# The last batch's PSUM banks, its maxima and the buffers around it laid out anew in an attention plus soft-MoE kernel

## The chip, the cores and the metric

The kernel runs on one NeuronCore of a Trainium2 chip. The engines that matter are PE (TensorE, with its weight loads shown apart as PEld), DVE (VectorE), ACT (ScalarE), POOL (GpSimd) and SP (SyncE, which here only issues DMAs). PE writes only to PSUM, which has eight banks of 512 float32 values on each of 128 partitions; DVE and ACT read PSUM and write SBUF; DMA moves data between HBM and SBUF.

The metric is the device time of one execution in microseconds. The time before is the median of three runs. Separately one execution was profiled; its span runs from its first to its last instruction.

## The reference

Twelve heads of causal attention over 8 batches of 448 tokens, followed by a soft mixture of 8 experts with 4 slots each. `x` is the attention output with all heads of a token side by side, 3584 tokens by 768.

```python
scores = np.where(mask, -1e9, q @ k.T / sqrt(64))
attn = np.exp(scores - scores.max(-1)); attn /= attn.sum(-1) + 1e-09
x = (attn @ v)                       # 8 x 448 tokens, 12 heads x 64 = 768 columns
logits = x @ phi                     # 3584 x 32 slots
d = np.exp(logits - logits.max(0)); d /= d.sum(0) + 1e-09      # over the tokens
slot_input = d.T @ x                 # 32 x 768, 4 slots for each of 8 experts
slot_out[e] = np.maximum(slot_input[e] @ w1[e], 0) @ w2[e]     # 768 -> 1024 -> 768
c = np.exp(logits - logits.max(1)); c /= c.sum(1) + 1e-09      # over the slots
out = c @ slot_out
```

The softmax `d` runs over all tokens, so no expert can start before the last batch's logits are known.

## The kernel before

**Attention.** The 96 heads (`NHD`) are worked off in one loop, `i` from 0 to 96, with an order written out by hand in `ORDER`; what is issued keeps program order on each engine (`_InOrder`). In step `i` PE makes the scores of head `i + 2` and `attv(i - 1)`, twenty products of the exponentials `pt_[(i-1) % 2]` with the values `va_`, into the PSUM tile `po0`; `norm` divides and stores into `x`. Pairs of heads `p = i // 2` share a column block of 128; six pairs make a batch. Three buffers `x_` hold three pairs each in turn, so the last batch lies in `x_[2]` (pairs 42 to 44) and `x_[0]` (pairs 45 to 47), and `x_[1]` holds the second half of the batch before. `plan` hangs the mixture's work on steps of the loop: `xtrans(p)` transposes a pair's `x` into an `xt` tile (PE, then an ACT copy), `logits_a` multiplies it with `phi`, `logits_b` takes the negated maximum of a batch and the running one, `logits_d` the exponentials, `dispatch` adds `d.T @ x` to the slot inputs `si`.

**The last batch.** Step 95 runs `attv(94)`, the plan's `xtrans(46)` and opens three score tiles as `ps`; step 96 runs `attv(95)` into `ps[0]`, of which lines 540 to 542 first clear a part, because the last chunk of tokens writes 65 rows. Lines 543 to 602 then finish batch 7 outside the loop:

- `lp` (in `ps[1]`) gets the partial logits `lt` by a product with the identity, pair 46's by `logits_a`, and pair 47's behind four transposes into `xp` (in `ps[2]`), which ACT copies out in one half (`xa`) and DVE in the other (`mx_`, the attention's buffer for maxima);
- `logits_b` and `logits_d` run on `lp`; `tm` takes the transposed running maximum, DVE reduces it over four groups of tokens into `nm` and copies it three times in one instruction; one product spreads it over the partitions, and `wc`, `rz`, `sidw` rescale the groups;
- `dispatch_a` multiplies into `sps` (right parts of `ps[2]` and `ps[0]`), `dispatch_b` adds into `si`, `tps` gathers the slot inputs into `slt`, and `zr` the denominators;
- the logits are copied to `lt`, transposed and copied to `lg[:, 7]`, which only the combine stage reads.

`warm(n, w)` issues `n` products whose result nobody reads, 512 columns wide, between these steps.

**Experts and output.** `expert_in(e)` is 24 x 4 products of `slt` with the first weights, `expert_out(e, hf)` 8 of the hidden values with the second; `combine` makes the output tiles in two halves of columns, and SP stores them.

**The weight stream.** `order` lists 64 weight loads, all issued by SP in program order, each into one tile of 1536 columns. Loads 0 to 21 go to `wres` during the attention. Loads 22 to 33 (line 678) go to the pool `wt1`, which takes the SBUF that `early.close()` frees: each load waits for the last use of whatever its 6144 bytes per partition lay on. Loads 34 to 63 reuse tiles 0 to 29 and wait for the expert products that read them. The pools on the right side lie one behind the other, later ones at lower addresses, tiles in the order of their declaration. Worked out from the declared sizes, the loads lie on these tiles before:

| load | lies on |
|---|---|
| 27 | `r2` of even pairs, `k2` of odd pairs |
| 28 | `k2`, `r2` of odd pairs, `mx` |
| 29 | `mx`, `mt`, `va0`, `pt0` |
| 30 | `pt0`, `va1`, `pt1` |
| 31 | `pt1`, small tiles, both `xt` |
| 32 | `xt`, `x1` |
| 33 | `x1`, `lt`, `x0` |
| 34 to 37 | weight tiles 0 to 3, read by `expert_in(0)` |

```python
    x_[1] = moe.tile([P, NCH, 3 * P], F32, name="x1")
    lt = moe.tile([P, P], F32, name="lt")
    x_[0] = moe.tile([P, NCH, 3 * P], F32, name="x0")
    x_[2] = moe.tile([P, NCH, 3 * P], F32, name="x2")
```

Of the kernel before, what the change touches and what calls it, by code (L numbers as in the profile page):

```python
# [9 lines left out]
F32 = mybir.dt.float32  # L10
# [24 lines left out]
WARM = (1, 2, 3, 1)  # L35
# [44 lines left out]
def attention_soft_moe(ctx: ExitStack, tc: tile.TileContext, qk, va, phi, w1, w2, out):  # L80
# [10 lines left out]
    ps_s = att.enter_context(tc.tile_pool(name="ps_s", bufs=3, space=PSUM))  # L91
    ps_1 = att.enter_context(tc.tile_pool(name="ps_1", bufs=1, space=PSUM))

# [8 lines left out]
    x_[1] = moe.tile([P, NCH, 3 * P], F32, name="x1")  # L102
# [75 lines left out]
    def warm(n, w=None):  # L178

        w = misc("warm") if w is None else w  # L180
        for _ in range(n):
            nc.tensor.matmul(w, identb, tri.unsqueeze(1).to_broadcast([P, 4, P]),
                             start=True, stop=True)
# [115 lines left out]
    def attv(i, qcs, first):  # L299
        if not 0 <= i < NHD:  # L300
            return
        p, h = divmod(i, 2)
        pt, v, po = pt_[i % 2], va_[p % 2], st.get(("po", i), po0)
        for qc in qcs:
            for c in range(qc + 1):
                col = SCOL[c] + P * (qc - c)


                m = P if qc < 3 else 65
                nc.tensor.matmul(po[0:m, qc], pt[:, col:col + m], v[:, c, h],  # L310
                                 start=c == 0 and qc in first, stop=c == qc, skip_group_check=True)
# [101 lines left out]
    for b in range(NB):  # L413
        o, last = 12 * b, b == NB - 1
        for j, r in enumerate((3, 5, 8, 9, 11, 13)):
            if not last or j < PPB - 1:
                plan[o + r] = lambda p=b * PPB + j: xtrans(p)
        plan[o + 10] = lambda b=b: next_logits(b, 2, misc(f"g{b}_2"))
        if not last:
            plan[o + 14] = lambda b=b: (next_logits(b, 4, misc(f"g{b}_4")), logits_b(b, lt))  # L420
            plan[o + 16] = lambda b=b: logits_e(b)
            plan[o + 18] = lambda b=b: dispatch(b, 0)
            plan[o + 19] = lambda b=b: dispatch(b, 1)
# [45 lines left out]

    def sid_part(g):  # L470
        nc.gpsimd.affine_select(out=sid, in_=sid, compare_op=ALU.not_equal, fill=1.0,
                                base=-32 * g, pattern=[[-1, NSLOT]], channel_multiplier=1)
# [4 lines left out]
    later += [lambda g=g: sid_part(g) for g in range(4)]  # L477

# [3 lines left out]
    for i in range(NHD + 1):  # L482
# [55 lines left out]
        if i == NHD - 1:  # L538

            ps = [ps_s.tile([P, 1024], F32, tag="s", name=f"e{k}") for k in range(3)]  # L540
            po = st["po", i] = ps[0][:, 0:NCH * VC].rearrange("p (c n) -> p c n", n=VC)
            nc.vector.memset(po[64:P, 3], 0.0)
    b = NB - 1
    lp, xp, tm, wm = ps[1][:, 0:P], ps[2][:, 0:512], misc("tm"), ps[1][:, 512:1024]

    nc.tensor.matmul(lp, ident, lt, start=True, stop=False, skip_group_check=True)
    logits_a(b, (4,), lp, first=False, last=False)
    warm(WARM[0], wm)
    x = st.pop(("x", NPAIR - 1))
    for c in range(NCH):  # L550
        nc.tensor.transpose(out=xp[:, P * c:P * c + P], in_=x[:, c], identity=ident)
    xa = xtp.tile([P, 512], F32, tag="xt", name="xta", bufs=2)
    nc.scalar.activation(out=xa[:, 0:256], in_=xp[:, 0:256], func=AF.Copy)
    nc.vector.tensor_copy(out=mx_[:, 0:256], in_=xp[:, 256:512])
    warm(WARM[1], wm)
    for c in range(NCH):
        nc.tensor.matmul(lp[32 * c:32 * c + 32], phis[1][:, 2], (xa if c < 2 else mx_)[:, P * (c % 2):P * (c % 2) + P],
                         start=False, stop=True, skip_group_check=True)
# [5 lines left out]
    nm = const.tile([1, 4, NSLOT], F32, name="nm")  # L564
    nc.vector.tensor_reduce(out=nm[:, 0], in_=tm[0:1, 0:P].rearrange("p (c s) -> p s c", s=NSLOT),
                            axis=AX.X, op=ALU.min)
    nc.vector.tensor_copy(out=nm[:, 1:4], in_=nm[:, 0:1].to_broadcast([1, 3, NSLOT]))
    nc.tensor.transpose(out=xp[:, 0:P], in_=gs, identity=ident)
    dn = st["dn", b] = gs.rearrange("p (c s) -> p c s", s=NSLOT)
    nc.scalar.activation(out=gs, in_=xp[:, 0:P], func=AF.Copy)  # L570
    nc.tensor.matmul(tm[:, P:P + 1], nm.rearrange("p c s -> p (c s)"), ident[0:1, 0:1], start=True, stop=True)
# [5 lines left out]
    sps = ps[2][:, 512:896], ps[0][:, 512:896]  # L577
# [7 lines left out]
    for hf in range(2):  # L585
        tps = (po0 if hf == 0 else po).rearrange("p a b->p (a b)")[:, 0:3 * NSLOT]
        for c in range(3):
            o = 384 * hf + P * c
            nc.tensor.matmul(tps[:, NSLOT * c:NSLOT * c + NSLOT], si[:, o:o + P], sidw,
                             start=True, stop=True)  # L590
        if hf == 0:
            nc.scalar.activation(out=slt[0], in_=tps, func=AF.Copy)
            zr = misc("zr")[:, 0:1]
            nc.tensor.matmul(zr, srep.rearrange("p a b->p (a b)"), rz, start=True, stop=True)
        else:
            nc.vector.tensor_copy(out=slt[1], in_=tps)

    nc.vector.tensor_scalar(out=rz, in0=zr, scalar1=EPS, scalar2=None, op0=ALU.add)
    nc.vector.reciprocal(out=rz, in_=rz)
    nc.scalar.activation(out=lt, in_=lp, func=AF.Copy)  # L600
    nc.tensor.transpose(out=xp[:, P:2 * P], in_=lt, identity=ident)
    nc.scalar.activation(out=lg[:, b], in_=xp[:, P:2 * P], func=AF.Copy)
# [126 lines left out]
    for e in range(NEXP):  # L729
        expert_in(e)  # L730
        loads(4)
# [66 lines left out]
```

## Time and profile before

| what | value |
|---|---|
| time, median of 3 runs | 467.52 us (466.68 to 469.02) |
| the profiled execution's own time | 468.74 us |
| its span | 467.0 us |
| PE, PEld busy | 428.3 us (92%), 363.3 us (78%) |
| DVE, ACT, POOL busy | 354.5, 329.8, 266.0 us |
| granted PE clock, mean | 0.983 |
| HBM read, written | 107.25 MB, 11.01 MB |

How to read it: busy shares are means over two stages. Up to about 360 us the attention keeps PE busy; behind it the weights and the output go through the DMA queue. The parts of the profile that carry the argument are quoted where it uses them. A row of the chain or the timeline gives the start in us, the duration in us, the engine and what is written from what; "x8" counts merged instructions, and the bracket behind gives the idle time before and what ended it. A row of a windows view gives the stretch, its length, then for PE, PEld, DVE, ACT and POOL the busy time with the number of instructions, the granted PE clock, the DMA share and GB/s.

### The profile page before, as it was taken

Reading aid. Unit: us, or ns where it says so; the run is one execution under the profiler, and the core shown is the slowest. Engines: PE = TensorE matmul, PEld = TensorE weight load, DVE = VectorE, ACT = ScalarE, POOL = GpSimd, SP = SyncE. Lnnn points to the kernel's source line nnn. Section 1 sums busy time; section 2 is a strip of 40 time slices with the busy share of each in tenths; the row PEclk is TensorE's granted clock in tenths of the full one; section 3 lists DMA queues with packets and bytes.
Section 4 is the critical chain, followed back from the end, with each engine's and each line's share of the span. In section 5 each row is a group of like instructions: output and inputs, shape, how many; then the busy total and the mean of one; then the engine's idle time right before and its main releaser. Section 6 shows DMA issues by size and latency. Waiting matters only on the chain.

```text
span 467.0 us, 11997 instructions
## 1 busy us (share of the span) xinstructions
PE 428.3 (92%) x4567; PEld 363.3 (78%) x4567; DVE 354.5 (76%) x1053; ACT 329.8 (71%) x489; POOL 266.0 (57%) x214
## 2 busy tenths in 40 slices
PE   6999999999999999999999999999999898976640
PEld 3699999999899989998999999899988454622220
DVE  5898899888988988898899888988985466322350
ACT  5798888889889979897888889789965111422240
POOL 4789778677777777876777777777771000000000
PEclk9999999999999999999999999999999999999985
DMA  7477766777667765767766677666748699999997
GB/s 240 130 253 233 231 193 222 230 232 218 198 207 233 236 225 171 242 217 232 215 216 201 225 234 232 204 197 223 247 149 314 239 413 413 416 414 413 403 394 287
DMA packets 38200, 119.03 MB, mean 255 GB/s; under 512 B 4096, under 2 KB 11776, under 8 KB 38144
## 3 DMA queue, kind: packets, MB, share of 16 engines
q1 hardware_dynamic: 38000, 118.01, 73.5%
q8 instruction: 36, 0.59, 0.5%
q10 hardware_dynamic: 144, 0.27, 0.1%
q14 instruction: 20, 0.16, 0.1%
HBM read 107.25 MB, written 11.01 MB: 253 GB/s over the span
## 4 chain that ended last, share of the span: by engine, by line
PE 68%; DMA 15%; ACT 5%; DVE 4%; issue 2%; POOL 1%; SPq 0%; ACTq 0%; POOLq 0%
PE po L64 29%; PE s L64 23%; DMA w<-in_w_dram 13%; PE xt L64 5%; PE sp L64 3%; PE g L64 2%; PE rt L64 2%; ACT pt L64 2%; DMA out_dram<-ot 2%; PE e L64 2%; ACT ks L64 2%; DMA qk<-in_qk_dram 1%; DVE mx L64 1%; PE pp L64 1%; ACT ot L64 1%
## 5 line engine op out<-in xcount | busy, mean ns | idle before, releaser
L64 PE MATMUL po<-va,pt 128*128 128x65 f32 x1900 | 193.6, 250 | 0.0
L64 PEld LDWEIGHTS po<-va,pt 128*128 128x128 f32 x1900 | 190.6, 171 | 0.3 <-DVE x L64 0.2
L64 DVE TENSOR_TENSOR mx<-s,mx 128x320 f32<-128x320 f32 (+2 forms) x288 | 100.8, 350 | 28.8 <-ACT mx L64 25.2
L64 POOL TENSOR_TENSOR r<-qk,qd 64x896 fp32r<-64x896 f32 (+1 forms) x50 | 101.4, 2029 | 7.6 <-ACT qd L64 3.8
L64 POOL TENSOR_SCALAR_AFFINE_SELECT r<-mr 14x448 fp32r<-14x448 f32 x96 | 61.4, 640 | 76.3 <-DVE mr L64 68.5
L64 ACT ACTIVATE pt<-s 128x1024 f32<-128x1024 f32 x96 | 98.0, 1021 | 7.4 <-PE s L64 3.8
L64 POOL TENSOR_TENSOR ks<-qk,ks 64x896 fp32r<-64x896 f32 (+1 forms) x47 | 98.0, 2084 | 5.0 <-ACT ks L64 1.4
L64 PE MATMUL s<-r,k 128*128 128x320 f32 (+3 forms) x384 | 83.2, 299 | 1.1 <-POOL r L64 1.1
L64 PE MATMUL s<-qd,ks 128*128 128x448 f32 (+3 forms) x384 | 78.0, 314 | 2.0 <-ACT qd L64 1.9
L64 ACT ACTIVATE mx<-s 128x448 f32<-128x448 f32 x96 | 52.4, 546 | 34.5 <-PE s L64 16.9
L64 DVE STREAM_TRANSPOSE mt<-mx 128x448 f32<-128x448 f32 x96 | 61.9, 645 | 3.3
L64 PEld LDWEIGHTS s<-r,k 128*128 128x128 f32 (+1 forms) x384 | 60.1, 176 | 5.2 <-issue 1.6
L64 PEld LDWEIGHTS s<-qd,ks 128*128 128x128 f32 (+1 forms) x384 | 56.3, 184 | 3.6 <-ACT qd L64 2.8
L64 DVE TENSOR_REDUCE r<-mt 128x14 f32<-128x448 f32 x96 | 58.4, 608 | 0.1
L64 ACT ACTIVATE ks<-qk 128x896 fp32r<-128x896 f32 (+1 forms) x50 | 45.6, 914 | 3.3 <-DMA qk<-in_qk_dram 3.3
L64 ACT ACTIVATE qd<-qk 128x896 fp32r<-128x896 f32 (+1 forms) x50 | 46.1, 923 | 0.9 <-DMA qk<-in_qk_dram 0.8
L64 ACT ACTIVATE k<-ks 64x896 fp32r<-64x896 f32 (+1 forms) x49 | 45.8, 934 | 1.1
L64 PEld LDWEIGHTS <-identb 128*128 128x128 bf16 x312 | 29.0, 103 | 19.1 <-issue 15.4
L64 DVE TENSOR_TENSOR x<-po,sm 128x256 f32<-128x256 f32 x95 | 40.3, 424 | 3.3
L64 PE MATMUL s<-tri,identb 128*128 128x64 bf16 (+2 forms) x288 | 40.3, 237 | 0.9
L64 PE MATMUL so<-w,ht 128*32 128x384 f32 x256 | 25.3, 493 | 9.4 <-DMA w<-in_w_dram 7.3
L64 ACT ACTIVATE xts<-xt 128x512 f32<-128x512 f32 x47 | 28.1, 598 | 7.2 <-PE xt L64 4.2
(129 smaller groups left out, 399.0 us busy)
## 6 DMA issues: line engine op xcount, KB each, us to landing
w<-in_w_dram SPq DMA_DIRECT2D x64, 768.0 KB, 9.0
qk<-in_qk_dram SPq DMA_DIRECT2D x94, 448.0 KB, 3.4
va<-in_va_dram SPq DMA_DIRECT2D x47, 260.0 KB, 3.5
out_dram<-ot SPq DMA_DIRECT2D x28, 384.0 KB, 6.6
qk<-in_qk_dram SPq DMA_DIRECT2D x4, 224.0 KB, 3.7
va<-in_va_dram ACTq DMA_DIRECT2D x1, 260.0 KB, 5.2
phi<-in_phi_dram SPq DMA_DIRECT2D x2, 48.0 KB, 3.7
```

The costliest lines, as they stand in the source:

```text
L64: return self._tc.keep_in_program_order(op(*args, **kwargs))
```

## The change

Everything lies in and around the last batch.

- **Banks.** The pool of the single PSUM tiles (`ps_1`) is declared ahead of the score tiles. After step 95 the score pool is closed and six single banks `e0` to `e5` are opened in its place: `xp` becomes two banks, `po`, `lp` and the two `sps` one each. `warm` writes into `po0`, 256 columns wide; `WARM` goes from 7 products in all to 15.
- **No memset.** In the last head the weights of the last chunk are 128 columns wide instead of 65, so that all rows are written, and the clearing goes.
- **Order.** `xtrans(46)` moves out of the plan of step 95 to behind `attv(95)`, and its `logits_a` behind the copies of pair 47.
- **Transposes in one buffer.** Both halves of pair 47's transposes go to `xa`; `mx_` isn't used there.
- **Maxima.** `nm` is 128 x 128, cleared once by POOL in a step of the loop; DVE writes its first row, and four products of 32 columns spread it in place of a copy and one product.
- **Late steps.** The last logits are copied to `nm` instead of `lt`; their transposition and the copy to `lg` move behind `expert_in(0)`, into a tile of the output pool; `zr` moves behind the slot inputs.
- **Layout.** `x1` moves from `moe` to the front of `xtp`. By the same arithmetic as above loads 28 to 30 lie where they lay; load 31 lies on `pt1`, small tiles and `x1`; load 32 on `x1` and both `xt`; load 33 on an `xt`, `lt` and `x0`.

```diff
-WARM = (1, 2, 3, 1)
+WARM = (3, 3, 6, 3)
...
-    ps_s = att.enter_context(tc.tile_pool(name="ps_s", bufs=3, space=PSUM))
     ps_1 = att.enter_context(tc.tile_pool(name="ps_1", bufs=1, space=PSUM))
+    scs = ExitStack()
+    ps_s = scs.enter_context(tc.tile_pool(name="ps_s", bufs=3, space=PSUM))
...
-    x_[1] = moe.tile([P, NCH, 3 * P], F32, name="x1")
+    x_[1] = xtp.tile([P, NCH, 3 * P], F32, name="x1")
...
-            nc.tensor.matmul(w, identb, tri.unsqueeze(1).to_broadcast([P, 4, P]),
+            nc.tensor.matmul(w, identb, tri.unsqueeze(1).to_broadcast([P, w.shape[1] // P, P]),
...
-                m = P if qc < 3 else 65
+                m = P if qc < 3 or i == NHD - 1 and c < 3 else 65
...
-            if not last or j < PPB - 1:
+            if not last or j < PPB - 2:
                 plan[o + r] = lambda p=b * PPB + j: xtrans(p)
...
+    nm = const.tile([P, P], F32, name="nm")
...
+    later += [lambda: nc.gpsimd.memset(nm[:, 0:NSLOT], 0.0)]
...
-            ps = [ps_s.tile([P, 1024], F32, tag="s", name=f"e{k}") for k in range(3)]
-            po = st["po", i] = ps[0][:, 0:NCH * VC].rearrange("p (c n) -> p c n", n=VC)
-            nc.vector.memset(po[64:P, 3], 0.0)
+            scs.close()
+            pe = att.enter_context(tc.tile_pool(name="pe", bufs=1, space=PSUM, reuse_waits="tile"))
+            ps = [pe.tile([P, 512], F32, name=f"e{k}") for k in range(6)]
+            po = st["po", i] = ps[2][:, 0:NCH * VC].rearrange("p (c n) -> p c n", n=VC)
     b = NB - 1
-    lp, xp, tm, wm = ps[1][:, 0:P], ps[2][:, 0:512], misc("tm"), ps[1][:, 512:1024]
+    xtrans(NPAIR - 2)
+    xp, lp, sps = ps[0:2], ps[3][:, 0:P], [ps[k][:, 0:384] for k in (4, 5)]
+    tm, wm = misc("tm"), po0.rearrange("p a b->p (a b)")[:, 0:2 * P]
 
     nc.tensor.matmul(lp, ident, lt, start=True, stop=False, skip_group_check=True)
-    logits_a(b, (4,), lp, first=False, last=False)
     warm(WARM[0], wm)
     x = st.pop(("x", NPAIR - 1))
     for c in range(NCH):
-        nc.tensor.transpose(out=xp[:, P * c:P * c + P], in_=x[:, c], identity=ident)
+        nc.tensor.transpose(out=xp[c // 2][:, P * (c % 2):P * (c % 2) + P], in_=x[:, c], identity=ident)
...
-    nc.scalar.activation(out=xa[:, 0:256], in_=xp[:, 0:256], func=AF.Copy)
-    nc.vector.tensor_copy(out=mx_[:, 0:256], in_=xp[:, 256:512])
+    nc.scalar.activation(out=xa[:, 0:256], in_=xp[0][:, 0:256], func=AF.Copy)
+    nc.vector.tensor_copy(out=xa[:, 256:512], in_=xp[1][:, 0:256])
+    logits_a(b, (4,), lp, first=False, last=False)
     warm(WARM[1], wm)
     for c in range(NCH):
-        nc.tensor.matmul(lp[32 * c:32 * c + 32], phis[1][:, 2], (xa if c < 2 else mx_)[:, P * (c % 2):P * (c % 2) + P],
+        nc.tensor.matmul(lp[32 * c:32 * c + 32], phis[1][:, 2], xa[:, P * c:P * c + P],
                          start=False, stop=True, skip_group_check=True)
...
-    nm = const.tile([1, 4, NSLOT], F32, name="nm")
-    nc.vector.tensor_reduce(out=nm[:, 0], in_=tm[0:1, 0:P].rearrange("p (c s) -> p s c", s=NSLOT),
+    nc.vector.tensor_reduce(out=nm[0:1, 0:NSLOT], in_=tm[0:1, 0:P].rearrange("p (c s) -> p s c", s=NSLOT),
                             axis=AX.X, op=ALU.min)
-    nc.vector.tensor_copy(out=nm[:, 1:4], in_=nm[:, 0:1].to_broadcast([1, 3, NSLOT]))
...
-    nc.tensor.matmul(tm[:, P:P + 1], nm.rearrange("p c s -> p (c s)"), ident[0:1, 0:1], start=True, stop=True)
+    for c in range(NCH):
+        nc.tensor.matmul(tm[32 * c:32 * c + 32, P:P + 1], nm[:, 0:NSLOT], ident[:, 0:1],
+                         start=True, stop=True, skip_group_check=True)
...
-    sps = ps[2][:, 512:896], ps[0][:, 512:896]
...
-            zr = misc("zr")[:, 0:1]
-            nc.tensor.matmul(zr, srep.rearrange("p a b->p (a b)"), rz, start=True, stop=True)
         else:
             nc.vector.tensor_copy(out=slt[1], in_=tps)
+    nc.scalar.activation(out=nm, in_=lp, func=AF.Copy)
+    zr = misc("zr")[:, 0:1]
+    nc.tensor.matmul(zr, srep.rearrange("p a b->p (a b)"), rz, start=True, stop=True)
...
-    nc.scalar.activation(out=lt, in_=lp, func=AF.Copy)
-    nc.tensor.transpose(out=xp[:, P:2 * P], in_=lt, identity=ident)
-    nc.scalar.activation(out=lg[:, b], in_=xp[:, P:2 * P], func=AF.Copy)
...
         expert_in(e)
+        if e == 0:
+            lgp = pso.tile([P, 512], F32, tag="o", name="lgp")
+            nc.tensor.transpose(out=lgp[:, 0:P], in_=nm, identity=ident)
+            nc.scalar.activation(out=lg[:, NB - 1], in_=lgp[:, 0:P], func=AF.Copy)
```

More of the change, by code (lines that the diff above doesn't have):

```diff
@@ L563, in attention_soft_moe @@
     logits_d(b, lp)
-    nm = const.tile([1, 4, NSLOT], F32, name="nm")
-    nc.vector.tensor_reduce(out=nm[:, 0], in_=tm[0:1, 0:P].rearrange("p (c s) -> p s c", s=NSLOT),
+    nc.vector.tensor_reduce(out=nm[0:1, 0:NSLOT], in_=tm[0:1, 0:P].rearrange("p (c s) -> p s c", s=NSLOT),
                             axis=AX.X, op=ALU.min)
-    nc.vector.tensor_copy(out=nm[:, 1:4], in_=nm[:, 0:1].to_broadcast([1, 3, NSLOT]))
-    nc.tensor.transpose(out=xp[:, 0:P], in_=gs, identity=ident)
+    nc.tensor.transpose(out=xp[0][:, 0:P], in_=gs, identity=ident)
     dn = st["dn", b] = gs.rearrange("p (c s) -> p c s", s=NSLOT)
-    nc.scalar.activation(out=gs, in_=xp[:, 0:P], func=AF.Copy)
-    nc.tensor.matmul(tm[:, P:P + 1], nm.rearrange("p c s -> p (c s)"), ident[0:1, 0:1], start=True, stop=True)
+    nc.scalar.activation(out=gs, in_=xp[0][:, 0:P], func=AF.Copy)
+    for c in range(NCH):
+        nc.tensor.matmul(tm[32 * c:32 * c + 32, P:P + 1], nm[:, 0:NSLOT], ident[:, 0:1],
+                         start=True, stop=True, skip_group_check=True)
     warm(WARM[3], wm)
```

## The prediction

> **What bounds the kernel now.** I read the page's slices first, for the rows that leave the attention's pattern.
>
> ```profile
> DMA  7477766777667765767766677666748699999997
> GB/s 240 130 253 233 231 193 222 230 232 218 198 207 233 236 225 171 242 217 232 215 216 201 225 234 232 204 197 223 247 149 314 239 413 413 416 414 413 403 394 287
> ```
>
> A slice is 11.7 us. From the 33rd (373.6 us) to the last the DMA share is 9 and the rate about 410 GB/s, while the 32nd, which holds the last batch, has 6 and 239 GB/s. So behind the last batch the queue is full, and in it there is a hole. Next come windows of that stretch, then the chain that ended last.
>
> ```profile
> 356.00:359.00 3.00, 3.00 (x42) 2.72 (x41) 0.96 (x4) 1.31 (x2) 0.38 (x1) 1.00 1.00 408
> 359.00:360.50 1.50, 0.84 (x8) 0.60 (x7) 0.88 (x4) 0.60 (x1) 0.00 (x0) 1.00 0.72 209
> 363.50:366.50 3.00, 2.40 (x18) 1.18 (x18) 0.88 (x3) 0.38 (x1) 0.00 (x0) 1.00 0.00 0
> 366.50:373.50 7.00, 6.10 (x66) 3.56 (x68) 3.26 (x14) 1.81 (x8) 0.00 (x0) 1.00 0.98 364
> 359.00:373.50 14.50, 12.23 (x120) 7.70 (x123) 5.78 (x24) 2.79 (x10) 0.00 (x0) 1.00 0.65 236
> 380.00:410.00 30.00, 28.15 (x412) 15.03 (x404) 17.20 (x59) 8.43 (x24) 0.00 (x0) 1.00 1.02 413
> 454.00:464.00 10.00, 0.00 (x0) 0.00 (x0) 0.00 (x0) 0.00 (x0) 0.00 (x0) 0.50 0.98 356
> ```
>
> ```profile
> 375.00 13.73 DMA w<-in_w_dram
> ...
> 434.24 7.83 DMA out_dram<-ot
> ```
>
> From 454 to 464 us no engine works and the DMA still stores at 356 GB/s: the end is the end of the queue's bytes. The chain says the same from 375 us on. Before 375 it runs over PE (`expert_in(0)`), but a queue that is full from there on has its time set by when bytes began to flow, not by `expert_in`. The hole is the thing to read: nothing moves from 363.5 to 366.5, and over 359 to 373.5 the mean is 236 GB/s, 3.42 MB. SP's waits name who holds the stream.
>
> ```profile
> SPq L64 <- DVE mx L64: 7.1, 1, 7.1
> SPq L64 <- PE e L64: 3.8, 2, 3.4
> ```
>
> ```profile
> 357.81 0.33 SPq L64 DMA_DIRECT2D w<-in_w_dram  x1
> 365.74 0.33 SPq L64 DMA_DIRECT2D w<-in_w_dram  x1
> 371.81 0.33 SPq L64 DMA_DIRECT2D w<-in_w_dram  x1
> 373.24 0.33 SPq L64 DMA_DIRECT2D w<-in_w_dram  x1
> ```
>
> These are loads 27, 28, 33 and 34 (counted from load 22, the first behind the last values' load). Load 28 lies on `mx`, which the last batch uses once more for pair 47's transposes, and waits 7.1 us for DVE's copy there and 0.4 for PE's reading of it. Loads 29 to 33 stand behind it in SP's order, whatever they lie on. Load 33 waits another 3.4 us, for the transposition of `lt`.
>
> **The change, the path first.** These are the steps of the last batch.
>
> ```profile
> 357.62 1.78 PE L64 MATMUL po<-va,pt 128*65 128x65 f32 x18
> 359.23 0.61 PE L64 MATMUL xt<-ident,x 128*128 128x128 f32 x4
> 360.35 0.11 DVE L64 MEMSET e<- 64x65 f32 x1
> 360.61 2.00 PE L64 MATMUL e<-va,pt 128*128 128x65 f32 x20 [0.77 <-ACT xts L64]
> 363.05 0.42 DVE L64 TENSOR_TENSOR x<-e,sm 128x256 f32<-128x256 f32 x1
> 363.62 0.63 PE L64 MATMUL e<-ident,x 128*128 128x128 f32 x4
> 364.35 0.38 ACT L64 ACTIVATE xta<-e 128x256 f32<-128x256 f32 x1 [3.88 <-PE e L64]
> 364.76 0.42 DVE L64 COPY mx<-e 128x256 f32<-128x256 f32 x1 [1.29 <-ACT xta L64]
> 365.24 0.41 PE L64 MATMUL e<-mx,phi 128*32 128x128 f32 x4
> 365.70 0.29 DVE L64 TENSOR_REDUCE bm<-e 128x1 f32<-128x128 f32 x1 [0.52 <-PE e L64]
> 366.05 0.81 PE L64 MATMUL e<-tri,identb 128*128 128x512 bf16 x3 [0.39 <-DVE bm L64]
> 366.90 0.37 ACT L64 ACTIVATE gs<-e,run_m 128x128 f32<-128x128 f32 x1 [2.17 <-PE e L64]
> 367.32 0.24 DVE L64 COPY nm<-nm 1x96 f32<-1x96 f32 x1
> 368.30 1.50 PE L64 MATMUL e<-x,gs 128*32 128x384 f32 x16
> 371.67 0.26 DVE L64 COPY slt<-e 128x96 f32<-128x96 f32 x1 [1.07 <-PE e L64]
> 372.14 5.39 PE L64 MATMUL hp<-w,slt 128*32 128x256 f32 x96 [0.37 <-ACT lg L64]
> ```
>
> - *No memset, `xtrans(46)` behind `attv(95)`.* `attv(95)` starts at 360.61, behind DVE's memset, which stands behind the normalization of head 94. Without it, it follows `attv(94)` at 359.40 and ends at 361.4, 1.2 us earlier; 128 columns in place of 65 cost nothing that shows (2.00 us for 20 products against 1.78 for 18). Pair 47's `x` is ready at about 362.3. Until then PE runs the moved `xtrans(46)` (0.6), the `lt` product (0.3) and three half-width warm products (half of 0.81: 0.4), to 362.6. So the transposes start 1.0 us earlier, at 362.6; `xtrans(46)` takes back 0.2.
> - *Two banks for `xp`.* Before, DVE's copy waited for ACT's: 1.56 us from the first transpose to its end. In two banks the copies overlap, about 1.1 us. Pair 46's logits (8 products, as long as the eight here: 0.8) and the warm products lie within that wait and beyond it by 0.2. The eight last products run as one group; `lp` is complete at about 364.4 instead of 365.65: 1.25 us earlier.
> - *Own banks for `lp` and warm.* Before, the warm products waited for `bm` and ran until 366.86, and `gs` waited for them although the running maximum follows `bm` (done at 365.99) by one short DVE step. In `po0` they wait for nobody: `gs` starts at about 364.95, 1.95 us earlier.
> - *Maxima by products.* The copy (0.24) goes; four products for one, each in two passes, are no row of this trace. Bounds: nothing, and 0.4 us as for the eight 128-column products above. I take 0.2, so the two cancel.
> - *The rest of the chain keeps its shape:* dispatch at 366.4 instead of 368.30, `slt` done at 369.7. `expert_in(0)` before stood until ACT's `lg` copy had left its bank, as its bracket says; that copy is gone from the path and `zr` (two products) runs while DVE copies `slt`. `expert_in(0)` starts at about 369.9: 2.2 us earlier. Behind it the late transposition costs PE 0.3 at most, beside a stage in which PE isn't the end.
> - *POOL's one more memset, the order of the PSUM pools:* no step waits for either. What stands behind the memset on POOL is `srep`, first read by `zr` hundreds of us later.
>
> **The stream.** With `mx` free since head 95's maxima, and `x1` (unused since the dispatch of the batch before) in the place of the `xt` tiles under load 31, the releases are:
>
> | load | waits for | issue before | issue after |
> |---|---|---|---|
> | 28 | `r2`, as load 27 | 365.74 | 358.3 |
> | 29 | `pt0`: `attv(94)` | behind 28 | 359.4 |
> | 30, 31 | `pt1`: `attv(95)` | behind 28 | 361.4, 361.9 |
> | 32 | `xt`: last logits | behind 28 | 364.4 |
> | 33 | `x0`: dispatch | 371.81 | 367.9 |
> | 34 | `expert_in(0)` | 373.24 | 371.0 |
>
> A load is 768 KB, 0.786 MB. Bytes come about 0.85 us after the issue (load 28 before: issued 365.74, nothing until 366.5). From 359 to 373.5 there are then at nearly all times two loads in flight or more. Two in flight moved 408 GB/s (356 to 359, loads 25 and 26), one alone 209. I take 0.25 MB to 360.2 as load 27 and 28 begin, 0.40 MB/us for the 13.3 us behind, and 0.1 less because load 33 is alone for a moment before 34: 5.5 MB in place of 3.42. The 2.1 MB are ahead of the queue when it reaches its steady 413 GB/s: 2.1 / 0.413 = 5.0 us.
>
> What is late next? The queue behind must stay full. Loads 34 to 41 are released by `expert_in(0)` and `(1)`, which the last row above merges: 5.39 us, for 8 x 0.786 / 0.413 = 15 us of transfer, so releases stay ahead. The second halves of the experts' outputs are where PE waits for weights before; PE gets there 2.2 us earlier, the weights 5.0.
>
> ```profile
> 413.46 0.85 PE L64 MATMUL so<-w,ht 128*32 128x384 f32 x8
> 415.27 0.85 PE L64 MATMUL so<-w,ht 128*32 128x384 f32 x8 [0.95 <-DMA w<-in_w_dram]
> 416.06 0.96 PE L64 MATMUL pp<-sr,ct 128*128 128x384 f32 x4
> 417.17 0.85 PE L64 MATMUL so<-w,ht 128*32 128x384 f32 x8 [0.15 <-DMA w<-in_w_dram]
> ```
>
> These are the second expert's rows and the first of the third. One takes 3.7 us (413.46 to 417.17) on the DMA's account; PE's own work is 0.85 + 0.85 + 0.96 = 2.7, so it makes up 1 us per expert and has caught up after three of the seven left. The end then moves with the queue. The sum against the profiled execution: span 467.0 - 5.0 = 462.0, its own time 468.74 - 5.0 = 463.7. That execution lies 1.2 above the median of the runs, so the median becomes 467.5 - 5.0 = 462.5 us.
>
> Bounds of this case: all 14.5 us at 413 GB/s give 5.99 MB, 6.2 us, 461.3. If the chain didn't move (loads 32 to 34 at about 365.7, 369.9 and 373.2) and two loads made only the 364 GB/s of the row from 366.5 on, 0.25 + 13.3 x 0.364 - 0.1 = 5.0 MB would move: 3.8 us, 463.7.
>
> **Rivals.**
>
> - *Only PE's 2.2 us count*, as the chain before 375 us would have it: 465.3. For it, PE is busy 28.15 of 30 us from 380 to 410; against it, the DMA is full there too and alone at the end.
> - *The layout frees nothing:* some tile under load 28 or 29 is still held up to the last logits. The stream restarts at 364.4 instead of 365.74 and load 34 comes at 371.0: about 1.5 us, 466.0. Against it, the table above finds no late reader.
> - *Early loads run singly at 209 GB/s:* 14.5 x 0.209 = 3.03 MB, 0.4 less than now, 0.9 us lost, 468.4. Against it, 408 GB/s with two in flight. The Trainium skill, "SBUF — State Buffer", section "The DMA setup-cost knee", has every transfer pay about 2 us that doesn't scale with bytes; were that paid in series, a load would take an estimated 3.8 us and the change would lose about 1 us. The 408 GB/s speak against that for loads that overlap.
> - *Slower: PE's clock.* After the last product (ended 450.16) the granted clock halves.
>
> ```profile
> 449.72 0.44 PE L64 MATMUL pp<-sr,ct 128*128 128x384 f32 x1 [0.20 <-ACT ot L64]
> ```
>
> ```profile
> 451.25:451.50 0.25, 0.00 (x0) 0.00 (x0) 0.00 (x0) 0.00 (x0) 0.00 (x0) 0.80 1.05 393
> 451.50:451.75 0.25, 0.00 (x0) 0.00 (x0) 0.00 (x0) 0.00 (x0) 0.00 (x0) 0.50 1.03 381
> ```
>
> That is about 1.2 us of idling. If the reordered steps with half-width warm products leave such a gap, the experts start at half clock. PE has some 8 us to spare at the end of the weights: 411.3 + 7 x 2.7 = 430 against 413.46 + 7 x 3.7 - 1 = 438 before. Half clock for 15 us of products adds 15, uses that up and ends 7 us later, 474.5; below 8 us it is not slower than before. Against it, I find no gap over 0.6 us in the new order, and 15 warm products of 256 columns are as much work as 7 of 512. The Trainium skill, "TensorE: Matmul & The Clock Gate", section "What's actually happening", lets the clock fall only after an idle window of about 3.4 us; the 1.2 us here are shorter, so I go by the row.
>
> **How the numbers follow.** Forecast 0.84; PE's 2.2 us alone 0.05; nothing freed 0.05; single loads 0.02; clock 0.04. The range starts at 461.3 less 0.5 for the runs' scatter, 460.8, and reaches to the second case, 465.3. About 0.5% (2.3 us) is what a measurement of this kernel can tell from no change. The forecast alone lies beyond it: faster 0.84; the three cases between are the same, 0.12; slower 0.04.
>
> **What would show it.** SP's wait for `mx` gone, load 28 issued within 1 us of load 27, no stretch at 0 GB/s between 359 and 372, some 5.5 MB moved from 359 to 373.5; `attv(95)` right behind `attv(94)`; the two copies of pair 47 overlapping; `expert_in(0)` near 369.9; PE waiting for weights again from the fourth expert of the second half. A release later than in the table, a granted clock below 1.00 at 370, or DMA falling short of 400 GB/s behind 374 would make it wrong.

## The result and the profile after

The changed kernel takes 462.22 us (median of 4 runs, 461.46 to 462.91), the kernel before 467.22 (4 runs, 466.68 to 469.02): a ratio of 0.9886 with a 95% interval of 0.9853 to 0.9919. The prediction said 462.5 and faster. The profiled execution took 461.80 us, its span is 460.1.

**A common clock first.** The profiled spans differ by 6.9 us, and not all of it is the change's. The last row reduction of the attention (head 95's, on POOL) is a mark that both kernels reach by the same steps. The timeline of the kernel before has it at

```profile
355.74 0.64 POOL L64 TENSOR_SCALAR_AFFINE_SELECT r<-mr 14x448 fp32r<-14x448 f32 x1 [2.39 <-DVE mr L64]
```

and that of the changed kernel at

```profile
354.28 0.64 POOL L64 TENSOR_SCALAR_AFFINE_SELECT r<-mr 14x448 fp32r<-14x448 f32 x1 [2.39 <-DVE mr L64]
```

Of the 1.46 us between them 1.4 are there within the first 20 us of the program, where the change touches nothing, and other executions of the changed kernel have the mark at 353.76 and 356.20. They are scatter of the start. What is left, 6.9 - 1.46 = 5.4 us, is the tail's own. "On before's clock" means below: a time of a profile less the distance of its mark from 355.74, so here plus 1.46.

**The stream.** The page's slices of the changed kernel:

```profile
DMA  7376666676567765776566766667648999999998
GB/s 267 112 273 236 222 205 219 225 234 219 191 205 255 234 211 173 236 251 217 192 209 217 233 234 206 214 215 236 227 158 285 374 407 413 416 414 414 401 395 301
```

The dip that the kernel before had in its 32nd slice (DMA 6, 239 GB/s) is gone: 9 and 374. Windows measure it. The first row, of the kernel before, is 359 to 380 us, which takes in the restart of the queue behind the hole:

```profile
359.00:380.00 21.00, 18.73 (x232) 11.38 (x235) 9.71 (x39) 3.41 (x12) 0.00 (x0) 1.00 0.76 292
```

Of the changed kernel the same 21 us on before's clock and the first 2 us of them, then three stretches on its own clock, and the stores at the end:

```profile
357.54:378.54 21.00, 20.72 (x282) 12.99 (x285) 11.47 (x45) 3.73 (x13) 0.00 (x0) 1.00 0.99 390
357.54:359.54 2.00, 2.00 (x21) 2.00 (x21) 0.77 (x3) 0.00 (x0) 0.00 (x0) 1.00 0.84 226
...
359.00:363.50 4.50, 4.50 (x49) 3.24 (x48) 1.64 (x6) 1.04 (x3) 0.00 (x0) 1.00 0.96 374
363.50:366.50 3.00, 2.72 (x31) 1.06 (x30) 1.60 (x7) 1.06 (x5) 0.00 (x0) 1.00 1.02 424
366.50:373.50 7.00, 7.00 (x111) 4.65 (x115) 3.48 (x15) 1.01 (x4) 0.00 (x0) 1.00 1.02 409
...
447.00:457.00 10.00, 0.00 (x0) 0.00 (x0) 0.00 (x0) 0.00 (x0) 0.00 (x0) 0.50 1.00 362
```

The last column times the length is what moved: 21 x 0.292 = 6.13 MB before, 21 x 0.390 = 8.19 after. The 2.06 MB more, at 0.413 MB/us, are 5.0 us, beside the 5.4 of the tail and the 5.0 of the medians. From 447 on no engine works and the stores still run at 362 GB/s: the end is still the end of the bytes. The 2 us at 226 GB/s are the start of loads 27 and 28: on before's clock they go out at 357.81 and 358.23, load 26 lands at about 360.0, and only from 361 on the rate is near 400 again, some 3 us behind the first issue. SP's waits in the last batch:

```profile
SPq L64 <- PE e L64: 5.4, 3, 3.1
SPq L64 <- PE hp L64: 3.8, 3, 2.4
SPq L64 <- DVE xta L64: 0.9, 1, 0.9
SPq L64 <- DVE x L64: 0.4, 1, 0.4
SPq L64 <- PE lgp L64: 0.3, 1, 0.3
```

No `mx`: the 7.1 us wait is gone. What remains are waits for steps of the last batch and of the first experts, 3.1 us at the longest. The issues of loads 27 and 28 (two rows of SP's timeline) now lie 0.42 us apart:

```profile
356.35 0.33 SPq L64 DMA_DIRECT2D w<-in_w_dram  x1
356.77 0.38 SPq L64 DMA_DIRECT2D w<-in_w_dram  x1
```

On before's clock the loads 28 to 34 go out at 358.23, 359.47, 361.59, 362.01, 364.36, 367.83 and 370.62; the prediction's table had 358.3, 359.4, 361.4, 361.9, 364.4, 367.9 and 371.0.

**The last batch on the engines** (timeline of the changed kernel, add 1.46 for before's clock):

```profile
356.16 1.78 PE L64 MATMUL po<-va,pt 128*65 128x65 f32 x18
357.77 2.29 PE L64 MATMUL e<-va,pt 128*128 128x65 f32 x20
...
360.99 0.66 PE L64 MATMUL e<-ident,x 128*128 128x128 f32 x4
...
364.21 0.24 PE L64 MATMUL tm<-ident,nm 128*32 128x1 f32 x8
...
364.82 1.50 PE L64 MATMUL e<-x,gs 128*32 128x384 f32 x16
...
368.06 2.80 PE L64 MATMUL hp<-w,slt 128*32 128x256 f32 x48
370.79 0.33 PE L64 MATMUL lgp<-ident,nm 128*128 128x128 f32 x1
```

```profile
361.53 0.38 ACT L64 ACTIVATE xta<-e 128x256 f32<-128x256 f32 x1 [0.39 <-PE e L64]
363.44 0.37 ACT L64 ACTIVATE gs<-e,run_m 128x128 f32<-128x128 f32 x1 [1.53 <-DVE run_m L64]
```

```profile
361.76 0.42 DVE L64 COPY xta<-e 128x256 f32<-128x256 f32 x1 [0.82 <-PE e L64]
...
367.97 0.26 DVE L64 COPY slt<-e 128x96 f32<-128x96 f32 x1 [0.85 <-PE e L64]
```

The brackets are what to look at. `attv(95)` has none and follows `attv(94)`; the copies of pair 47 overlap (361.53 to 361.91 on ACT, 361.76 to 362.18 on DVE); the first expert starts without a wait. Its 24 products (6 x 4, not 24 x 4) are the 48 records of the `hp` row, two passes each.

**Behind it.** The chain that ended last is DMA from 372.76 on, as it was from 375.00 before:

```profile
371.12 1.48 PE hp L64 x24
372.76 12.84 DMA w<-in_w_dram
```

and in the second half of the experts' outputs PE soon runs into the weights:

```profile
407.07 1.50 PE L64 MATMUL so<-w,ht 128*32 128x384 f32 x16
408.50 0.97 PE L64 MATMUL pp<-sr,ct 128*128 128x384 f32 x4
409.40 1.50 PE L64 MATMUL so<-w,ht 128*32 128x384 f32 x16
...
414.21 0.85 PE L64 MATMUL so<-w,ht 128*32 128x384 f32 x8
416.09 0.85 PE L64 MATMUL so<-w,ht 128*32 128x384 f32 x8 [1.03 <-DMA w<-in_w_dram]
```

One expert takes PE 2.33 us (407.07 to 409.40) while it is behind. The row at 414.21 is the fourth expert's (the third's, at 411.74, is left out); from 416.09 on PE waits a microsecond for each pair of loads.

### The profile page after: what moved, and what is told of

Its sections match the earlier page's. It is cut to its first block, busy times and chain, and to the rows that moved or that the text cites. A ratio compares the mean times of both kernels' runs of the same rounds, so it can differ in the third digit from the quotient of the medians.

```text
span 460.1 us, 12026 instructions
## 1 busy us (share of the span) xinstructions
PE 426.2 (93%) x4581; PEld 363.3 (79%) x4581; DVE 354.2 (77%) x1051; ACT 329.7 (72%) x489; POOL 266.1 (58%) x215
## 4 chain that ended last, share of the span: by engine, by line
PE 68%; DMA 14%; DVE 6%; ACT 5%; issue 3%; POOL 1%; SPq 0%; ACTq 0%; POOLq 0%
PE po L64 29%; PE s L64 23%; DMA w<-in_w_dram 13%; PE xt L64 5%; PE sp L64 3%; PE g L64 2%; ACT pt L64 2%; PE rt L64 2%; ACT ks L64 2%; DVE mx L64 1%; PE e L64 1%; PE pp L64 1%; DMA qk<-in_qk_dram 1%; DVE run_z L64 1%; PE hp L64 1%
```

## The experiments

The theory: time is won by the bytes that the queue moves before it is full for good, each 0.413 MB worth 1 us. The rivals: the earlier start of the experts (PE), the place of `x1`, the warm products (PE's clock). For every run I give the GB/s of 359 to 380 on before's clock, since that is where the theory puts the gain. "Before" is each time the kernel before, run beside it.

**One buffer alone, in the kernel before.**

```diff
-    nc.vector.tensor_copy(out=mx_[:, 0:256], in_=xp[:, 256:512])
+    nc.vector.tensor_copy(out=xa[:, 256:512], in_=xp[:, 256:512])
...
-        nc.tensor.matmul(lp[32 * c:32 * c + 32], phis[1][:, 2], (xa if c < 2 else mx_)[:, P * (c % 2):P * (c % 2) + P],
+        nc.tensor.matmul(lp[32 * c:32 * c + 32], phis[1][:, 2], xa[:, P * c:P * c + P],
```

> The kernel before with one line of the change: both halves of pair 47's transposes go to xa, mx stays out of it. The stream theory (the gain is DMA time won in the hole behind load 27): loads 28, 29, 30 go out near 358.3, 359.5 and 362.7 on the clock of before, 31 and 32 still wait for the last logits (365.7), 33 for the late lt (371.8). The queue runs dry shortly ahead of 33. 4.7 to 4.8 MB move from 359 to 373.5 instead of 3.42: 3.0 to 3.3 us gained, about 464.1 us. The rival (the gain is PE's earlier expert_in(0)): expert_in(0) does not move, so no gain, 467.2.

Measured: 465.88 us beside 467.4; ratio 0.9963 (0.9944 to 0.9981), 1.5 us by the medians. Its windows, 359 to 380 and then the last 6.5 us of these on before's clock, and its first expert:

```profile
357.94:378.94 21.00, 18.72 (x232) 11.36 (x235) 9.71 (x39) 3.41 (x12) 0.00 (x0) 1.00 0.91 328
372.44:378.94 6.50, 6.50 (x120) 3.67 (x116) 3.94 (x15) 0.62 (x2) 0.00 (x0) 1.00 0.87 300
```

```profile
371.08 4.29 PE L64 MATMUL hp<-w,slt 128*32 128x256 f32 x74 [0.37 <-ACT lg L64]
```

The first expert stands at mark + 16.40 us, exactly as before (372.14 - 355.74), and still the kernel is faster: bytes count and not PE's start. But I had expected about twice as much. The second row shows why: loads 33 and 34 still go out late (371.8 and 373.24), so the queue has nearly run dry once more (139 GB/s from 375 to 376) and moves only 300 GB/s behind 373.5, where the kernel before moved 416. My account had ended at 373.5, too early. Over 359 to 380 the gain is 21 x (0.328 - 0.292) = 0.76 MB, 1.8 us, about what was measured.

**All of the memory part, in the kernel before:** the above, `x1` moved to `xtp`, and the last logits copied to a tile of their own instead of `lt`.

```diff
-    x_[1] = moe.tile([P, NCH, 3 * P], F32, name="x1")
+    x_[1] = xtp.tile([P, NCH, 3 * P], F32, name="x1")
...
-    nm = const.tile([1, 4, NSLOT], F32, name="nm")
+    nq = const.tile([P, P], F32, name="nq")
+    nm = nq[0:1].rearrange("p (c s) -> p c s", s=NSLOT)
...
-    nc.scalar.activation(out=lt, in_=lp, func=AF.Copy)
-    nc.tensor.transpose(out=xp[:, P:2 * P], in_=lt, identity=ident)
+    nc.scalar.activation(out=nq, in_=lp, func=AF.Copy)
+    nc.tensor.transpose(out=xp[:, P:2 * P], in_=nq, identity=ident)
```

> The kernel before with only the change's memory: xa for both halves, x1 in front of the xt tiles, the last logits copied to a tile of their own instead of lt. Banks, order, memset, maxima as before. Stream theory: load 31 goes out with 30 near 363, 32 at 365.7, 33 behind the dispatch near 369.9 instead of 371.8, 34 at 373.2. About 5.0 MB in the window: 3.8 us gained, 463.4 us. The rival: expert_in(0) stays near 372.1, no gain, 467.2.

Measured: 464.47 us; ratio 0.9938 (0.9914 to 0.9962), 2.9 us (1.8 to 4.0), again less than expected and for the same reason. The profiled execution is the slowest of the ten (467.35).

```profile
359.03:380.03 21.00, 18.73 (x232) 11.37 (x235) 9.70 (x39) 3.41 (x12) 0.00 (x0) 1.00 0.96 361
373.53:380.03 6.50, 6.50 (x120) 3.67 (x116) 3.93 (x15) 0.62 (x2) 0.00 (x0) 1.00 0.94 338
```

By bytes 21 x (0.361 - 0.292) = 1.45 MB, 3.5 us. The first expert starts where it started (372.17, mark 355.77). Load 34 still comes at 373.24, and the queue is short of work around it: 338 GB/s. So by the bytes (1.45 of 2.06 MB) and by the medians the layout alone gives over half of the gain, and the shorter chain is needed for the rest.

**The changed kernel with the second half back in `mx`:** all of the change but the release of `mx`; `x1` and the late logits stay as changed.

```diff
-    nc.vector.tensor_copy(out=xa[:, 256:512], in_=xp[1][:, 0:256])
+    nc.vector.tensor_copy(out=mx_[:, 0:256], in_=xp[1][:, 0:256])
...
-        nc.tensor.matmul(lp[32 * c:32 * c + 32], phis[1][:, 2], xa[:, P * c:P * c + P],
+        nc.tensor.matmul(lp[32 * c:32 * c + 32], phis[1][:, 2], (xa if c < 2 else mx_)[:, P * (c % 2):P * (c % 2) + P],
```

> The changed kernel with one thing undone: the second half of pair 47's transposes goes to mx again, so load 28 waits for the last logits. The chain of the last batch stays as short as in the changed kernel (expert_in(0) 2.6 us earlier than before by the profile). Stream theory: the hole stays, from about 363 to 365, and ends 1.4 us earlier than before; with 33 no longer late some 1.5 us gained, 465.7 us. The rival: PE's 2.6 us count, 464.6 us.

Measured: 465.52 us; ratio 0.9962 (0.9943 to 0.9981), 1.9 us by the medians.

```profile
SPq L64 <- DVE mx L64: 5.4, 1, 5.4
```

```profile
357.25:378.25 21.00, 20.72 (x282) 12.96 (x285) 11.47 (x45) 3.73 (x13) 0.00 (x0) 1.00 0.83 316
371.75:378.25 6.50, 6.50 (x116) 3.41 (x112) 4.93 (x21) 0.93 (x3) 0.00 (x0) 1.00 1.02 413
```

SP waits for `mx` again, and 24 GB/s more than before make 0.50 MB, 1.2 us. The experts start as early as in the changed kernel (367.77, mark + 13.78), and that alone does not give its time. By the medians 1.9 us (0.9 to 2.7) does not quite exclude the rival's 2.6; but the 1.2 us by bytes and the 1.5 us by which the profile is shorter from its mark to its end lie nearer the 1.5 expected from the stream. Here the queue is full behind 373.5 (413 GB/s), the opposite of the two runs above: the hole in front and the shortage behind have different causes, the `mx` wait and the late release of loads 33 and 34.

**The changed kernel again,** beside these three.

> The changed kernel unchanged, beside the three others on one chip. Both theories: 462.2 us, 5.0 us faster than before.

Measured: 463.0 us; ratio 0.9905 (0.9878 to 0.9932); 389 GB/s over 359 to 380, 8.17 MB. This profile showed something else, the windows of the second half's start:

```profile
434.00:435.00 1.00, 0.51 (x1) 0.00 (x0) 0.00 (x0) 0.45 (x1) 0.00 (x0) 0.50 1.07 401
...
438.00:440.00 2.00, 2.00 (x7) 1.18 (x6) 1.45 (x3) 1.18 (x4) 0.00 (x0) 0.50 1.07 400
```

The granted clock halves at 434 and the output products run late, but the DMA's rate in the last column stays at about 400. The last PSUM copy of this profile (mark 353.76), and behind it that of the first profile of the changed kernel (mark 354.28):

```profile
445.42 0.56 DVE L64 COPY ot<-pp 128x384 f32<-128x384 f32 x1 [0.18 <-PE pp L64]
```

```profile
443.29 0.56 DVE L64 COPY ot<-pp 128x384 f32<-128x384 f32 x1 [0.18 <-PE pp L64]
```

It comes 2.65 us later behind the mark, the end of the span only 0.9. PE's delay reaches the end in a third, as it should where the end is the end of the bytes: a test by accident, in one execution.

**PE's chain made late, the layout as changed.**

```diff
+    warm(20, wm)
     for hf in range(2):
         dispatch_a(b, hf, sps[hf])
```

> The changed kernel with 20 more warm products of 256 columns ahead of the dispatch of the last batch: PE reaches the dispatch and expert_in(0) about 2.2 us later, the loads 28 to 32 go out as in the changed kernel, 33 and 34 about 2.2 us later. Stream theory: 34 comes at about 372.8 on before's clock instead of 370.6, after 32 has been read (at about 371), so the queue runs low for 1.5 to 2 us and makes a ramp: 0.4 to 0.9 MB less up to 380, 1 to 2 us slower than the changed kernel (463.5 to 465). Rival (the end follows PE): 2.2 us slower, and the rows of the second half show PE never waiting for weights. What tells them apart best is the bytes moved from 359 to 380 on before's clock, which the stream theory divides by 0.413 MB/us.

Measured: 463.96 us beside 467.06; ratio 0.9935 (0.9916 to 0.9955). The three other variants of this series lie at 462.0 to 462.3, so the delay costs 1.6 to 1.9.

```profile
358.72:379.72 21.00, 20.74 (x258) 13.82 (x261) 9.59 (x37) 3.42 (x12) 0.00 (x0) 0.95 0.98 368
```

The expected 0.4 MB is there: 21 x (0.390 - 0.368) = 0.46 MB, 1.1 us. Loads 28 to 31 go out as in the changed kernel, 33 and 34 at 370.16 and 372.97 instead of 367.83 and 370.62. That is 2.3 us and not 2.2; this execution's granted clock is 0.95, which may be the rest. PE meets the weights again in the second half (4.1 us of waits for loads between 405 and 440), so up to there PE does not set the time. By the medians alone 1.6 to 1.9 cannot be told from the rival's 2.2; the bytes and the waits speak for the stream.

**More work for PE where the queue is full:** four warm products of 512 columns behind each expert's second half.

```diff
         expert_out(e, 1)
+        warm(4, pt2.tile([P, 512], F32, tag="h", name=f"fl{e}"))
```

> The changed kernel with four warm products of 512 columns behind the second output half of each expert: some 0.85 us more PE work for each of eight experts, 6 to 7 us in all, all of it behind the first half of the weight loads. Stream theory (the end is the end of the queue's bytes, PE has spare time at 2.33 us of work for 3.75 us of weights): within 0.5 us of the changed kernel. Rival (PE sets the end): about 6 us slower.

Measured: 462.32 us; ratio 0.991 (0.988 to 0.994). The timeline:

```profile
409.88 1.50 PE L64 MATMUL so<-w,ht 128*32 128x384 f32 x16
411.31 1.04 PE L64 MATMUL fl<-tri,identb 128*128 128x512 bf16 x4
...
412.97 1.50 PE L64 MATMUL so<-w,ht 128*32 128x384 f32 x16
```

An expert now takes PE 3.09 us instead of 2.33, some 6 us over eight experts, and nothing of it is seen in the time. The rival in which PE sets the end, worth 6 us here, falls, though only for PE's work behind 410 us; what lies ahead of that the late chain tests. PE merely meets the weights one expert later (at the fifth, 423.50, instead of the fourth).

**The place of `x1` undone.**

```diff
-    x_[1] = xtp.tile([P, NCH, 3 * P], F32, name="x1")
+    x_[1] = moe.tile([P, NCH, 3 * P], F32, name="x1")
```

> The changed kernel with x1 back where it lay, so that load 31 lies on the xt tiles again and waits for the last logits. On before's clock loads 31 and 32 go out at about 364.4 and 364.8 instead of 362.0 and 364.4. Stream theory: loads 29 and 30 are in flight until about 364.5, the queue runs with two or one load for a short time; 0 to 0.3 MB less, 0 to 0.7 us slower than the changed kernel. Rival (the place of x1 is what frees the stream): load 31 missing for 2.4 us costs 2.4 x 0.413 = 1 MB, 2.4 us.

Measured: 462.02 us; ratio 0.9898 (0.988 to 0.9916).

```profile
357.31:378.31 21.00, 20.72 (x282) 12.98 (x285) 11.46 (x45) 3.73 (x13) 0.00 (x0) 1.00 0.98 389
```

Load 31 goes out at 364.36 instead of 362.01, and nothing is lost (389 against 390 GB/s): loads 29 and 30 are still in flight and land at about 368.0 and 369.9. This part of the change is worth nothing that can be measured.

**No warm products in the last batch.**

```diff
-WARM = (3, 3, 6, 3)
+WARM = (0, 0, 0, 0)
```

> The changed kernel without the fifteen warm products of the last batch. Clock rival: the idle gaps of PE between the steps add up to a fall of the granted clock, the experts start below 1.00, expert_in(0) takes longer than 2.8 us, load 34 comes later and the time rises by 1 to 7 us. Against it: no gap is longer than about 0.7 us, and after the last product the clock fell only after about 1.2 us; then the clock stays 1.00, expert_in(0) starts up to 0.3 us earlier and the time is that of the changed kernel within 0.5 us.

Measured: 462.21 us; ratio 0.9908 (0.9882 to 0.9934).

```profile
360.99 0.66 PE L64 MATMUL e<-ident,x 128*128 128x128 f32 x4 [0.26 <-DVE x L64]
...
363.32 0.27 PE L64 MATMUL tm<-ident,run_m 128*1 128x128 f32 x1 [0.68 <-DVE run_m L64]
...
367.72 2.80 PE L64 MATMUL hp<-w,slt 128*32 128x256 f32 x48
```

The largest wait that appears is 0.68 us, the granted clock is 1.00 from 357 to 440 and the experts' products keep their 2.80 us. The clock rival has no place in the last batch, with or without warm products.

**What is left of the dip.** In all runs of the changed kernel 359 to 363.5 stays at 319 to 334 GB/s on before's clock. Load 27 goes out only at 357.81 there, because it lies on `k2` of odd pairs, which the scores of head 95 read to the end. A variant of the changed kernel puts `mx` and `mt`, free earlier, in that place:

```diff
-    mx_ = wk.tile([P, S], F32, name="mx")
-    mt_ = wk.tile([P, S], F32, name="mt")
...
-    ops = [[fix.tile([P, 2, S], F32R, name=f"{o}{i}") for o in ("k2", "r2")] for i in range(NR)]
+    ops = []
+    for i in range(NR):
+        ops.append([fix.tile([P, 2, S], F32R, name=f"{o}{i}") for o in ("k2", "r2")])
+        if i == 0:
+            mx_ = fix.tile([P, S], F32, name="mx")
+            mt_ = fix.tile([P, S], F32, name="mt")
```

> The changed kernel with mx and mt declared between the two pairs' k2 and r2 tiles, so that load 27 no longer lies on k2 of odd pairs, which the scores of head 95 read to the end, but on r2 of even pairs, mx and mt; k2 and r2 of odd pairs move under the loads 28 and 29. On before's clock load 27 goes out at about 355 instead of 357.81, right behind the row reduction of head 95; 28 and 29 stay at about 358.2 and 359.5. Stream theory: what the changed kernel still lacks is the dip of 359 to 363.5 (319 to 334 GB/s against 413, 0.36 to 0.42 MB); it goes, 1.0 us at most, so 461.2 to 461.8 beside the changed kernel's 462.2. Rival (the dip is the end of the attention's own traffic and not load 27's lateness): the dip and the time stay.

> The changed kernel once more, as the neighbour of the kernel above: 462 to 463 us, some 8.2 MB moved from 359 to 380 on before's clock.

Measured: the variant 460.7 us (459.75 to 461.62, 6 runs), the changed kernel beside it 463.56 (462.07 to 464.96, 7 runs), the kernel before 467.51; the ratios to before are 0.9859 (0.9827 to 0.9891) and 0.9908 (0.9874 to 0.9943). Both miss what was expected, the variant below its 461.2 to 461.8 and the changed kernel above its 462 to 463. Load 27's issue, the whole stretch and the former dip in the variant (its mark is at 353.44, so plus 2.30 for before's clock):

```profile
352.44 0.34 SPq L64 DMA_DIRECT2D w<-in_w_dram  x1
```

```profile
356.70:377.70 21.00, 20.71 (x282) 12.99 (x285) 11.47 (x45) 3.73 (x13) 0.00 (x0) 1.00 1.01 411
...
356.70:361.20 4.50, 4.50 (x46) 3.90 (x46) 1.81 (x7) 0.98 (x2) 0.00 (x0) 1.00 1.00 400
```

Load 27 goes out at 354.74, the dip is filled (400 GB/s against 320 in the neighbour's profile), so it was not the end of the attention's traffic, and 411 GB/s over 21 us is about what the full queue moves (413). By bytes that is 21 x (0.411 - 0.388) = 0.48 MB, 1.2 us, and from mark to end of span the variant takes 104.96 us against 105.90. The medians differ by 2.9; the 1.7 beyond the bytes are not explained by the stream. Of the 3.7 us between the two profiled spans 2.76 lie ahead of the marks. The variant's one profile has the earliest mark of all (353.44 against 353.76 to 356.20 in three of the changed kernel), so a part may be the scatter of the start or an attention that runs a little better in this layout; this stays open. The variant is the fastest kernel of this study by its median; what its layout is shown to give is about 1 us.

Over all kernels, gain against before in us (bytes: the GB/s of 359 to 380 less 292, times 21, over 413; tail: how much shorter than the 111.26 us of before the profile is from the mark to the end of its span):

| kernel | GB/s | by bytes | tail | measured, medians |
|---|---|---|---|---|
| one buffer alone | 328 | 1.8 | 1.6 | 1.5 |
| memory part alone | 361 | 3.5 | 1.4 | 2.9 |
| all but the `mx` release | 316 | 1.2 | 1.5 | 1.9 |
| changed, chain late | 368 | 3.9 | 3.8 | 3.1 |
| changed, three profiles | 390, 389, 388 | 5.0, 4.9, 4.9 | 5.4, 4.5, 5.4 | 5.0, 4.4, 4.0 |
| changed, filler | 380 | 4.5 | 4.7 | 4.7 |
| changed, `x1` back | 389 | 4.9 | 5.1 | 5.0 |
| changed, no warm | 394 | 5.2 | 5.2 | 4.9 |
| variant, `mx` between | 411 | 6.1 | 6.3 | 6.8 |

The medians of nine kernels follow the bytes within 1 us, about the scatter of their medians, and the tails within 0.5, but for one: the memory part's profile moves only 371 and 337 GB/s in 440 to 460 us, where the kernel before moves 399 and 371, so that 0.6 MB or 1.5 of the 2.1 us missing in its tail go at the stores. From 359 us to the end all twelve profiles move the same 40.2 to 40.4 MB. PE's start does not order the kernels: the first two start the experts as late as before.

## Why the prediction was right

- **The bound.** Named from the page as the end of the queue's bytes, with `mx` holding load 28. Shown by the filler (6 us of PE work, no change), by the halved clock in one execution (2.65 us later on PE, 0.9 at the end) and by one buffer alone (faster with the experts' start unmoved).
- **The releases.** Six of the table's seven times hold within 0.2 us; load 34 comes 0.4 early. `attv(95)` at 359.23 on before's clock (predicted 359.40), the transposes at 362.45 (362.6), `gs` at 364.90 (364.95), dispatch at 366.28 (366.4), the second `slt` copy done at 369.69 (369.7). The four spreading products took 0.24 (0.2 was taken between nothing and 0.4), the late transposition 0.33 (0.3). One term was put at nothing and is not: with 128 columns throughout, `attv(95)` takes 2.29 us instead of 2.00. The two rows that were compared both mixed widths. As it starts 0.17 earlier than forecast, it ends at 361.52, near the 361.4 of the sum.
- **The step of the chain that was off** is the start of the experts: 369.52 instead of 369.9. I let it wait for DVE's copy of the second `slt`; but the first half of its products reads only the first, which ACT has copied at 367.55, and PE starts at 368.06, 0.17 before DVE is done at 368.23. The chain is shortened by 2.6 us, not 2.2, and load 34 comes 0.4 earlier.
- **The bytes.** 5.5 MB were predicted for 359 to 373.5; on before's clock 5.57, 5.51 and 5.50 moved in three profiles. The total is right by two terms that miss in opposite directions: 319 to 334 GB/s moved up to 363.5 (1.44 MB in the first profile, drawn 1.57), then 381 to 419 (4.13 MB, drawn 3.90). The reading behind it, two loads in flight make 408 GB/s and one alone 209, does not hold. Before, load 26 was in flight until about 360.1, most of the row that was read as one load alone; in the changed kernel two and more loads were in flight from 359 to 361 and moved 226. What the traces show is a delay of about 3 us from an issue into an emptying queue to the full rate: 357.81 to 361 here, and before from load 28's issue at 365.74 to about 369.
- **The catch-up.** Predicted: waiting again from the fourth expert. So it was, but in part by luck. An expert costs PE 2.33 us and not 2.7: the sum 0.85 + 0.85 + 0.96 counted the modelled tail of each row, while sixteen products in one row take 1.50 and the next row begins 0.07 before that one's end (408.50 against 408.57). So PE makes up 1.4 us per expert and not 1, on weights that come 5.3 us earlier (417.55 against 422.84 at the fourth expert) while PE comes 2.6 earlier. At 1 us, three of the seven experts behind the first would have put the first wait at the fifth.
- **The rivals.** "Only PE's 2.2 us" would have left PE never waiting for weights, and it waits. "The layout frees nothing" is refuted by load 28 at 358.23. "Early loads run singly" was wrong in its condition, two and more are in flight, yet a slow start did cost what the variant wins back. The clock rival finds no gap. Its 1.2 us of idling is no fixed limit either: the clock fell about 1.2 us behind the last product in the first profile of the changed kernel too, but 1.5 in the third and 4.2 with `x1` back. Ranged at 460.8 to 465.3, all three medians of the changed kernel (462.22, 463.0, 463.56) lie inside, two of them above the forecast.

What the experiments add is that the parts of the change don't simply add up. The release of `mx` is worth 0.76 MB in the kernel before, and with all else changed 1.56 (2.06 less 0.50): it fills the hole in front, but only with a shorter chain and a free `lt` do loads 33 and 34 come in time to keep the queue from running low behind it. So the account has to run on until the queue is full again.

## What to carry to other kernels

Where a queue issues in order over memory that earlier stages still use, list for each transfer the last reader of what it lies on: one late reader blocks everything behind it, and where tiles lie is as good a lever as when they are used. Count the gain in bytes up to the point where the queue stays full, not up to the end of the hole. Then look at the next dip with the same list; here moving two more tiles made the kernel faster once again.

## What was not expected of the hardware

- **The clock can halve amid work.** In the second profile of the changed kernel PE's granted clock fell to 0.50 at 434 us and stayed there to 440, with no wait on PE longer than 1.04 us in the 14 us before. Three variants show it too, for about 3 us each and behind waits of at most 1.2 us: `mx` between (from 433.4), the late chain (from 437.6) and the filler (from 440.5). In the five other profiles of the changed kernel and its variants it stayed at 1.00 until PE's last product. One of these waits in PE's timeline of the second profile:

```profile
431.68 0.85 PE L64 MATMUL so<-w,ht 128*32 128x384 f32 x8 [1.04 <-DMA w<-in_w_dram]
```

The Trainium skill, "TensorE: Matmul & The Clock Gate", section "HAM oscillation — how this bites in real kernels", asks only for no idle gaps over about 3.4 us. Here the clock fell behind nothing longer than repeated waits of about 1 us, in four executions and not in five others, which that rule does not cover; what set it off stays open.

- **A lower clock for a whole execution.** The profile of the late chain shows 0.95 in all stretches up to 437 us. The 20 products of `attv(95)` took 2.30 us against 2.29, the 48 records of an expert 2.90 against 2.80, and its mark (355.46) lies among the others'. An effect on the attention does not show beside the scatter of the marks.
- **The stores' rate scatters.** 362 GB/s at the end of the changed kernel's first profile (447 to 457), 335 in the memory part's (450 to 460), without any engine at work: over 10 us that is 0.7 us of time, as much as some of the effects measured here.
- **The start scatters by up to 2.4 us** among three profiles of one kernel (marks 353.76 to 356.20; the filler's, the same up to there, is at 357.09), and so do the times. A mark inside the program, and bytes or distances counted from it, resolve what the medians leave unclear.
